# Reordering Q.K and P.V around the exponential in a 32-head attention kernel, with a shorter prologue and finish

## The chip, the cores and the metric

The kernel runs on one core of a Trainium2 chip. The metric is the device time of one launch in microseconds (us), measured over several launches; the profile is one further execution, whose span (first to last instruction) is about 1.8 us shorter than the timed value. Launches of one kernel agree within 0.13%.

Engines: TensorE does matrix products (PE in the profile, PEld its weight loads), ScalarE (ACT) the exponentials, VectorE (DVE) the small elementwise work, and the SyncE queue (SP) starts the DMA transfers.

## The reference

```python
B, H, S, D = 1, 32, 2048, 640      # Dh = D // H = 20
def reference(q, k, v, t):          # q, k, v: [1, 32, 2048, 20] bf16; t: [32]
    qn = q / (jnp.sqrt((q * q).sum(axis=-1, keepdims=True)) + 1e-6)
    kn = k / (jnp.sqrt((k * k).sum(axis=-1, keepdims=True)) + 1e-6)
    logits = jnp.einsum('bhqd,bhkd->bhqk', qn, kn) * t[None, :, None, None]
    attn = softmax(logits, axis=-1)
    return jnp.einsum('bhqk,bhkd->bhqd', attn, v)
```

Normalised rows make the logits small, so the kernel takes the exponential without subtracting a maximum. A column of ones beside V gives the denominators.

## The kernel before

The score matrix of a head (2048 keys x 2048 queries) is cut into 64 units of 128 keys x 512 queries. Three units make a *wave*: three Q.K matmuls write 3 x 512 columns of PSUM (`psS`, two slots), one activation takes the exponential of all 1536 columns into SBUF (`p_slot`, two slots), and three P.V matmuls add the result to the head's accumulator (`psO`). There are 683 waves. The heads have no gap between them: a wave may hold the end of one and the start of the next.

```python
def pe_qk(eng, w):                  # on TensorE
    slot = w % 2
    ...                             # first unit of a head: wait for the transposed q and k
    for i, uu in enumerate(us):
        ...
        last = eng.matmul(dst, lhsT, rhs, tile_position=(32 * g, 0))      # K = 20 rows
    last.then_inc(s_qk, 1)

def pe_pv(eng, w):
    ...                             # first unit of a head: zero its psO bank by a matmul with zeros
    eng.wait_ge(s_act, w + 1)       # activation w is done
    for i, uu in enumerate(us):
        ...
        last = eng.matmul(dst, lhsT, rhs, ..., tile_position=(0, 32 * g))  # 32 columns wide
    last.then_inc(s_pv, 1)

# ScalarE, for every wave w
eng.wait_ge(s_qk, w + 1)
eng.activation(p_slot[:, slot, ...], psS[slot ...], ACT.Exp).then_inc(s_act, 1)

# TensorE's program
for w in range(NW):
    pe_qk(eng, w)
    if w >= 1:
        pe_pv(eng, w - 1)
    if w in fin_at_wave:            # waves 4 to 7 of the next head:
        n, c = fin_at_wave[w]
        pe_fin_transposes(eng, n, c, c)   # four small transposes of head n's accumulator
```

Seen from the moment at which activation w-1 ends, TensorE does P.V(w-1), then perhaps four transposes, then Q.K(w+1). Activation w+1 needs that Q.K.

Per head, VectorE prepares q (square, sum, reciprocal square root in ten small steps, scale), then k in the same way with its own ten steps, and writes the normalised k four times into `kn_rep`; two DMA transposes then make `qTg` and `kT`. At the end of a head VectorE copies the accumulator to SBUF, TensorE transposes it back into PSUM, VectorE copies that to `fin_sb`, divides and stores.

Of the kernel before, what the change touches and what calls it, by code (L numbers as in the profile page):

```python
# [14 lines left out]
def bass_standalone__qk_norm__prompt_kernel(  # L15
# [28 lines left out]
    def first_wave_of_head(h):  # L44
        return (h * NU) // WAVE

    NB = 5
    NT = 2

    with ExitStack() as es:  # L50
# [10 lines left out]
        rqt_all = sbuf("rqt_all", [128, H, R], F32)  # L61
        rs_u = sbuf("rs_u", [128, R], I32)
        rs_a = sbuf("rs_a", [128, R], F32)
        rs_b = sbuf("rs_b", [128, R], F32)
        rs_c = sbuf("rs_c", [128, R], F32)
        rs_y = sbuf("rs_y", [128, R], F32)

# [10 lines left out]

        p_slot = sbuf("p_slot", [128, 2, WAVE * 512], BF16)

        acc_sb = sbuf("acc_sb", [128, 512], F32)
        fin_sb = sbuf("fin_sb", [128, 512], F32)
        rsum_rec = sbuf("rsum_rec", [128, R], F32)
# [10 lines left out]
        s_Tq = [sem(f"s_Tq{i}") for i in range(NT)]  # L94
        s_Tk = [sem(f"s_Tk{i}") for i in range(NT)]
        s_out = [sem(f"s_out{i}") for i in range(2)]
# [15 lines left out]
        def out_count_before(n):  # L112
            return n // 2

        def ld_count(n):
            return 16 * (n // NB + 1)

        def issue_loads(eng, n):
            b = n % NB
            if n >= NB:  # L120
                eng.wait_ge(s_pv, waves_done_through_head(n - NB))
            src_q = q[0, n].rearrange("(p r) d -> p r d", p=128)
            src_k = k[0, n].rearrange("(p r) d -> p r d", p=128)
            src_v = v[0, n].rearrange("(p r) d -> p r d", p=128)
            eng.dma_start(q_sb[b][:, :, :], src_q).then_inc(s_ldq[b], 16)
            eng.dma_start(k_sb[b][:, :, :], src_k).then_inc(s_ldk[b], 16)
            eng.dma_start(vaug[b][:, :, 0:D], src_v).then_inc(s_ldv[b], 16)

        def issue_transposes(eng, n):
            b = n % NB  # L130
            b2 = n % NT
            eng.wait_ge(s_prep, 2 * n + 1)
            if n >= NT:
                eng.wait_ge(s_qk, waves_done_through_head(n - NT))
            src = qn_pad[b][:, :, :].rearrange("p r d -> p (r d)")
            dst = qTg[b2][:, :].rearrange("p (c n) -> p c n", n=128)
            eng.dma_start_transpose(dst, src).then_inc(s_Tq[b2], 16)
            eng.wait_ge(s_prep, 2 * n + 2)
            src = kn_rep[b][:, :, :, :].rearrange("p r g d -> p (r g d)")
            dst = kT4[b2][:, :].rearrange("p (r n) -> p r n", n=128)  # L140
            eng.dma_start_transpose(dst, src).then_inc(s_Tk[b2], 16)

# [6 lines left out]
        @blk.sync  # L149
        def _(eng: bass.BassEngine):  # L150
            issue_loads(eng, 0)
            src_t = bass.AP(t.tensor, 0, [[0, 128], [1, H]])
            eng.dma_start(tb16[:, :], src_t).then_inc(s_tld, 16)
            if H > 1:
                issue_loads(eng, 1)
            for n in range(H):
                issue_transposes(eng, n)
                if n >= 2:
                    issue_out(eng, n - 2)
                if n + 2 < H:  # L160
                    issue_loads(eng, n + 2)
            for n in range(max(0, H - 2), H):
                issue_out(eng, n)
            n0 = (H + 1) // 2
            n1 = H // 2
            if n0 > 0:
                eng.wait_ge(s_out[0], 16 * n0)
            if n1 > 0:
                eng.wait_ge(s_out[1], 16 * n1)
# [6 lines left out]
        @blk.scalar  # L176
        def _(eng: bass.BassEngine):
            eng.wait_ge(s_init, 1)
            eng.activation(act_scr[:, :], act_scr[:, :], ACT.Exp)
            for w in range(NW):  # L180
                n_u = len(waves[w])
                slot = w % 2
                eng.wait_ge(s_qk, w + 1)
                src = psS[:, slot * WAVE * 512:slot * WAVE * 512 + n_u * 512]
                dst = p_slot[:, slot, 0:n_u * 512]
                eng.activation(dst, src, ACT.Exp).then_inc(s_act, 1)  # L186
# [45 lines left out]
        def dve_prep(eng, n):  # L232
            b = n % NB
            eng.wait_ge(s_ldq[b], ld_count(n))
            dve_wait_prev(eng)
            dop(eng, eng.tensor_tensor(sq_q[b][:, :, :], q_sb[b][:, :, :], q_sb[b][:, :, :], ALU.mult))  # L236
            dve_wait_prev(eng)
            dop(eng, eng.tensor_reduce(sums_all[:, n, 0:R], sq_q[b][:, :, :], AXIS_X, ALU.add))  # L238
            dve_rsqrt(eng, rinv_all[:, n, 0:R], sums_all[:, n, 0:R])
            if n == 0:  # L240
                eng.wait_ge(s_tld, 16)
                dve_wait_prev(eng)
                dop(eng, eng.tensor_copy(t_f32[:, :], tb16[:, :]))
            dve_wait_prev(eng)
            dop(eng, eng.tensor_scalar(rqt_all[:, n, :], rinv_all[:, n, 0:R],
                                      t_f32[:, n:n + 1], None, ALU.mult))
            dve_wait_prev(eng)
            rq = bcast_d(rqt_all[:, n, :])
            dop(eng, eng.tensor_tensor(qn_pad[b][:, :, 0:D], q_sb[b][:, :, :], rq, ALU.mult), ext=s_prep)  # L249
            eng.wait_ge(s_ldk[b], ld_count(n))  # L250
            dve_wait_prev(eng)
            dop(eng, eng.tensor_tensor(sq_k[b][:, :, :], k_sb[b][:, :, :], k_sb[b][:, :, :], ALU.mult))  # L252
            dve_wait_prev(eng)
            dop(eng, eng.tensor_reduce(sums_all[:, n, R:2 * R], sq_k[b][:, :, :], AXIS_X, ALU.add))  # L254
            dve_rsqrt(eng, rinv_all[:, n, R:2 * R], sums_all[:, n, R:2 * R])
            rk = bcast_d(rinv_all[:, n, R:2 * R])
            for g in range(NG):
                dve_wait_prev(eng)
                ins = eng.tensor_tensor(kn_rep[b][:, :, g, 0:D], k_sb[b][:, :, :], rk, ALU.mult)  # L259
                dve_chain(ins, ext=(s_prep if g == NG - 1 else None))  # L260

        def dve_fin(eng, n):
            b2 = n % 2
            eng.wait_ge(s_pv, waves_done_through_head(n))
            if n >= 1:
                eng.wait_ge(s_finT, 4 * n)
            dve_wait_prev(eng)
            dop(eng, eng.tensor_copy(acc_sb[:, :], psO[:, b2 * 512:(b2 + 1) * 512]), ext=s_fincopy)  # L268
            eng.wait_ge(s_finT, 4 * (n + 1))
            if n >= 2:  # L270
                eng.wait_ge(s_out[b2], 16 * out_count_before(n))
            dve_wait_prev(eng)
            dop(eng, eng.tensor_copy(fin_sb[:, :], psO[:, b2 * 512:(b2 + 1) * 512]))  # L273
            dve_wait_prev(eng)
            den = bass.AP(fin_sb, D, [fin_sb[:, :].ap[0], [32, R], [1, 1]])
            dop(eng, eng.reciprocal(rsum_rec[:, :], den))
            dve_wait_prev(eng)
            fin = bass.AP(fin_sb, 0, [fin_sb[:, :].ap[0], [32, R], [1, D]])
            rec_b = bass.AP(rsum_rec, 0, [rsum_rec[:, :].ap[0], [1, R], [0, D]])
# [33 lines left out]

        qk_waited_heads = set()
        pv_started_heads = set()

        def pe_qk(eng, w):
            slot = w % 2
            us = waves[w]
            for uu in us:  # L320
# [3 lines left out]
                if h not in qk_waited_heads:  # L324
                    eng.wait_ge(s_Tq[b2], 16 * (m2 + 1))
                    eng.wait_ge(s_Tk[b2], 16 * (m2 + 1))
                    qk_waited_heads.add(h)
            last = None
            for i, uu in enumerate(us):
# [8 lines left out]
        def pe_pv(eng, w):  # L338
# [14 lines left out]
            for i, uu in enumerate(us):  # L353
# [3 lines left out]
                lhsT = vaug[b][:, r, :]  # L357
                rhs = p_slot[:, slot, i * 512:(i + 1) * 512]
                dst = psO[32 * g:32 * g + 32, b2 * 512:(b2 + 1) * 512]
# [3 lines left out]

        def pe_fin_transposes(eng, n, g, chunk):
            b2 = n % 2
            if chunk == 0:
                eng.wait_ge(s_fincopy, n + 1)
            else:
                eng.wait_ge(s_finT, 4 * n + chunk)
            last = None  # L370
            for r in (g, g + 4, g + 8, g + 12):
                c = r // NG
# [7 lines left out]
        for n in range(H - 1):  # L380
            wb = first_wave_of_head(n + 1)
            for c in range(4):
                fin_at_wave[wb + 4 + c] = (n, c)

        @blk.tensor
        def _(eng: bass.BassEngine):
            for w in range(NW):
                pe_qk(eng, w)
                if w >= 1:
                    pe_pv(eng, w - 1)  # L390
                if w in fin_at_wave:
                    n, c = fin_at_wave[w]
                    pe_fin_transposes(eng, n, c, c)
            pe_pv(eng, NW - 1)
            for c in range(4):
                pe_fin_transposes(eng, H - 1, c, c)

# [27 lines left out]
```

## Time and profile before

The time before is 981.9 us. The following lines are from the page of the kernel before: the busy time of each engine (share of the span, number of instructions).

```profile
span 980.1 us, 11528 instructions
...
PE 832.1 (85%) x4640; PEld 198.5 (20%) x4640; DVE 333.0 (34%) x1115; ACT 935.7 (95%) x685; POOL 0.4 (0%) x5
```

The costliest groups of the kernel before. Columns: line, engine, operation, output<-inputs, shapes, count | busy us, mean ns of one | idle time of the engine just before them, and what ended it.

```profile
L186 ACT ACTIVATE p_slot<-psS 128x1536 bf16<-128x1536 f32 (+1 forms) x683 | 934.2, 1447 | 35.9 <-PE psS L335 31.1
L360 PE MATMUL psO<-p_slot,vaug 128*32 128x512 bf16 x2048 | 419.5, 608 | 126.7 <-ACT p_slot L186 125.4
L335 PE MATMUL psS<-qTg,kT 20*128 20x512 bf16 x2048 | 447.8, 602 | 16.6 <-DMA kT<-kn_rep 16.6
```

Up to the tail of 7.7 us, ScalarE's 683 activations fill the span except for 35.9 us, of which 15.0 are the start. TensorE, ahead of P.V, waits for ScalarE 125.4 us in all. The chain that ended last names TensorE too:

```profile
ACT 78%; PE 20%; DVE 1%; issue 1%; DMA 1%; ACTq 0%; DVEq 0%
```

Next, the timeline of the kernel before at a plain wave and at a wave with transposes (start us, duration us, engine, line, operation; in brackets the idle time before).

```profile
489.82 0.61 PE L360 MATMUL psO<-p_slot,vaug 128*32 128x512 bf16 x3 [0.21 <-ACT p_slot L186]
490.37 0.61 PE L335 MATMUL psS<-qTg,kT 20*128 20x512 bf16 x3
491.16 0.61 PE L360 MATMUL psO<-p_slot,vaug 128*32 128x512 bf16 x3 [0.18 <-ACT p_slot L186]
...
499.43 0.61 PE L360 MATMUL psO<-p_slot,vaug 128*32 128x512 bf16 x3 [0.18 <-ACT p_slot L186]
499.98 0.29 PE L376 MATMUL psO<-idn,acc_sb 21*128 21x21 f32 x1
499.99 0.61 PE L335 MATMUL psS<-qTg,kT 20*128 20x512 bf16 x2
500.10 0.48 PE L376 MATMUL psO<-idn,acc_sb 21*128 21x21 f32 x3
500.42 0.59 PE L335 MATMUL psS<-qTg,kT 20*128 20x512 bf16 x1
...
501.05 2.98 ACT L186 ACTIVATE p_slot<-psS 128x1536 bf16<-128x1536 f32 x2 [0.31 <-PE psS L335]
```

In a plain wave Q.K comes 0.55 us after P.V. With transposes its last matmul comes 0.99 us after P.V (500.42 against 499.43), and ScalarE stands idle for 0.31 us.

### The profile page before, as it was taken

To read this page: it belongs to the slowest core of one execution; us is meant where nothing else is said; L and a number is where in the kernel's file an instruction comes from. 1 tells how busy PE (TensorE), PEld (TensorE's weight loads), DVE (VectorE), ACT (ScalarE), POOL (GpSimd) and SP (SyncE) were. 2 spreads that over 40 slices of the span, in tenths; PEclk is the share of its full clock that TensorE was granted. 3 is DMA by queue.
4 is the path that set the end of the run, shared out by engine and by line. 5 is a ranking of instruction groups with operands and counts; after the bars stand their busy time and mean duration, and the time that the engine had idled before them with its cause. 6 is when DMAs were issued, how large, how long until landed. Compare 5 with 4: busy or idle time off the path is not lost.

```text
span 980.1 us, 11528 instructions
## 1 busy us (share of the span) xinstructions
PE 832.1 (85%) x4640; PEld 198.5 (20%) x4640; DVE 333.0 (34%) x1115; ACT 935.7 (95%) x685; POOL 0.4 (0%) x5
## 2 busy tenths in 40 slices
PE   2888888888888888888888888889888888888887
PEld 0122221222211222212222112222112222122221
DVE  8733134342234331334423343413343223430000
ACT  3999999999999999999999999999999999999996
POOL 0000000000000000000000000000000000000000
DMA  4212212122121122121221121321211222201100
GB/s 63 44 30 41 39 29 41 19 36 41 36 33 32 23 41 41 27 41 19 36 41 38 30 37 17 41 41 28 41 26 29 41 40 28 41 14 31 31 1 7
DMA packets 164037, 32.21 MB, mean 33 GB/s; under 512 B 151696, under 2 KB 163984, under 8 KB 163984
## 3 DMA queue, kind: packets, MB, share of 16 engines
q1 hardware_dynamic: 163984, 31.48, 19.5%
q8 instruction: 36, 0.59, 0.3%
q14 instruction: 17, 0.14, 0.1%
HBM read 7.87 MB, written 2.62 MB: 11 GB/s over the span
## 4 chain that ended last, share of the span: by engine, by line
ACT 78%; PE 20%; DVE 1%; issue 1%; DMA 1%; ACTq 0%; DVEq 0%
ACT p_slot L186 78%; PE psS L335 8%; PE psO L360 8%; PE psO L376 3%; PE psO L311 1%; DMA kT<-kn_rep 0%; DVE kn_rep L259 0%; DMA q_sb<-in_q_dram 0%; ACTq L50 0%; DVE rs_a L221 0%; DVE rs_b L223 0%; DVE rs_c L225 0%; DVE fin_sb L273 0%; DVE acc_sb L268 0%; DVE sq_q L236 0%
## 5 line engine op out<-in xcount | busy, mean ns | idle before, releaser
L186 ACT ACTIVATE p_slot<-psS 128x1536 bf16<-128x1536 f32 (+1 forms) x683 | 934.2, 1447 | 35.9 <-PE psS L335 31.1
L360 PE MATMUL psO<-p_slot,vaug 128*32 128x512 bf16 x2048 | 419.5, 608 | 126.7 <-ACT p_slot L186 125.4
L335 PE MATMUL psS<-qTg,kT 20*128 20x512 bf16 x2048 | 447.8, 602 | 16.6 <-DMA kT<-kn_rep 16.6
L360 PEld LDWEIGHTS psO<-p_slot,vaug 128*32 128x32 bf16 x2048 | 73.3, 101 | 461.2 <-ACT p_slot L186 461.2
L335 PEld LDWEIGHTS psS<-qTg,kT 20*128 20x128 bf16 x2048 | 90.1, 102 | 260.2 <-issue 260.2
L273 DVE COPY fin_sb<-psO 128x512 f32<-128x512 f32 x32 | 22.1, 692 | 281.0 <-PE psO L376 281.0
L268 DVE COPY acc_sb<-psO 128x512 f32<-128x512 f32 x32 | 22.1, 691 | 251.3 <-PE psO L360 251.3
L376 PE MATMUL psO<-idn,acc_sb 21*128 21x21 f32 x512 | 78.3, 276 | 1.0 <-DVE acc_sb L268 0.8
L376 PEld LDWEIGHTS psO<-idn,acc_sb 21*128 21x128 f32 x512 | 63.7, 209 | 56.0 <-issue 54.2
L259 DVE TENSOR_TENSOR kn_rep<-k_sb,rinv_all 128x320 bf16<-128x320 bf16 x128 | 63.0, 492 | 4.4
L236 DVE TENSOR_TENSOR sq_q<-q_sb 128x320 f32<-128x320 bf16 x32 | 15.8, 492 | 75.2 <-DMA q_sb<-in_q_dram 74.5
L223 DVE TENSOR_TENSOR rs_b<-rs_a,sums_all 128x16 f32<-128x16 f32 x128 | 22.3, 174 | 4.4
L225 DVE TENSOR_SCALAR rs_c<-rs_b 128x16 f32<-128x16 f32 x128 | 22.3, 174 | 4.4
L311 PE MATMUL psO<-zt 32*128 32x512 bf16 x32 | 19.9, 621 | 0.0
L252 DVE TENSOR_TENSOR sq_k<-k_sb 128x320 f32<-128x320 bf16 x32 | 15.7, 492 | 3.3
L249 DVE TENSOR_TENSOR qn_pad<-q_sb,rqt_all 128x320 bf16<-128x320 bf16 x32 | 15.7, 492 | 1.1
L281 DVE TENSOR_TENSOR o_stage<-fin_sb,rsum_rec 128x320 bf16<-128x320 f32 x32 | 15.7, 491 | 1.1
L238 DVE TENSOR_REDUCE sums_all<-sq_q 128x16 f32<-128x320 f32 x32 | 15.6, 486 | 1.1
L254 DVE TENSOR_REDUCE sums_all<-sq_k 128x16 f32<-128x320 f32 x32 | 15.5, 486 | 1.1
L221 DVE TENSOR_TENSOR rs_a<-rs_u 128x16 f32<-128x16 f32 x64 | 11.2, 175 | 2.2
L229 DVE TENSOR_TENSOR rs_y<-rs_u,rs_c 128x16 f32<-128x16 f32 x64 | 11.2, 174 | 2.2
L221 DVE TENSOR_TENSOR rs_a<-rs_y 128x16 f32<-128x16 f32 x64 | 11.2, 174 | 2.2
(21 smaller groups left out, 59.5 us busy)
## 6 DMA issues: line engine op xcount, KB each, us to landing
q_sb<-in_q_dram SPq DMA_DIRECT2D x32, 80.0 KB, 2.0
k_sb<-in_k_dram SPq DMA_DIRECT2D x32, 80.0 KB, 2.1
vaug<-in_v_dram SPq DMA_DIRECT2D x32, 80.0 KB, 3.1
out_dram<-o_stage SPq DMA_DIRECT2D x32, 80.0 KB, 1.6
qTg<-qn_pad SPq DMA_TRANSPOSE x32, 2.4
kT<-kn_rep SPq DMA_TRANSPOSE x32, 4.3
tb<-in_t_dram SPq DMA_DIRECT2D x1, 8.0 KB, 3.4
```

Source lines behind the costliest of these rows:

```text
L186: eng.activation(dst, src, ACT.Exp).then_inc(s_act, 1)
L221: dop(eng, eng.tensor_tensor(rs_a[:, :], cur, cur, ALU.mult))
L223: dop(eng, eng.tensor_tensor(rs_b[:, :], rs_a[:, :], src, ALU.mult))
L225: dop(eng, eng.tensor_scalar(rs_c[:, :], rs_b[:, :], -0.5, 1.5, ALU.mult, ALU.add))
L236: dop(eng, eng.tensor_tensor(sq_q[b][:, :, :], q_sb[b][:, :, :], q_sb[b][:, :, :], ALU.mult))
L259: ins = eng.tensor_tensor(kn_rep[b][:, :, g, 0:D], k_sb[b][:, :, :], rk, ALU.mult)
L268: dop(eng, eng.tensor_copy(acc_sb[:, :], psO[:, b2 * 512:(b2 + 1) * 512]), ext=s_fincopy)
L273: dop(eng, eng.tensor_copy(fin_sb[:, :], psO[:, b2 * 512:(b2 + 1) * 512]))
L311: eng.matmul(psO[:, b2 * 512:(b2 + 1) * 512], zt[0:32, 0:128], zt[0:32, 0:512], start=True, stop=True)
L335: last = eng.matmul(dst, lhsT, rhs, tile_position=(32 * g, 0))
L360: last = eng.matmul(dst, lhsT, rhs, start=False, stop=False, skip_group_check=True, tile_position=(0, 32 * g))
L376: last = eng.transpose(dst, lhsT, rhs, tile_position=(32 * g, 0))
```

## The change

The intent: keep ScalarE fed. (1) TensorE does Q.K(w) first after activation w-2 and P.V(w-2) behind it; P gets a third buffer, because activation w may now start before P.V(w-2) has read its input. (2) The transposes of a finished head are spread over eight waves, two in each. (3) The prologue of each head is shorter: q and k share one reciprocal square root, and k's transpose is split so that the first quarter can be used early; in the first head t is also loaded ahead of v. (4) The finish reads PSUM directly instead of through `fin_sb`. The core of the diff:

```diff
+    KA = 4
-        p_slot = sbuf("p_slot", [128, 2, WAVE * 512], BF16)
+        p_slot = sbuf("p_slot", [128, 3, WAVE * 512], BF16)
-                dst = p_slot[:, slot, 0:n_u * 512]
+                dst = p_slot[:, w % 3, 0:n_u * 512]
 ...                                                   # transposes: 2 in 8 waves, not 4 in 4
+            return [(g, g + 8) for g in range(NG)] + [(g + 4, g + 12) for g in range(NG)]
 ...                                                   # k's DMA transpose in two parts
+            src = kn_rep[b][:, 0:KA, :, :].rearrange("p r g d -> p (r g d)")
+            eng.dma_start_transpose(dst, src).then_inc(s_TkA[b2], 16)
+            src = kn_rep[b][:, KA:R, :, :].rearrange("p r g d -> p (r g d)")
+            eng.dma_start_transpose(dst, src).then_inc(s_TkB[b2], 16)
 ...                                                   # one root for q and k; k is squared first
-            dve_rsqrt(eng, rinv_all[:, n, 0:R], sums_all[:, n, 0:R])
+            dve_rsqrt(eng, rinv_all[:, n, :], sums_all[:, n, :])
 ...                                                   # kn_rep: two instructions in place of four
 ...                                                   # finish
-            dop(eng, eng.tensor_copy(fin_sb[:, :], psO[:, b2 * 512:(b2 + 1) * 512]))
-            den = bass.AP(fin_sb, D, [fin_sb[:, :].ap[0], [32, R], [1, 1]])
+            den = bass.AP(psO, b2 * 512 + D, [psO[:, :].ap[0], [32, R], [1, 1]])
 ...                                                   # TensorE's program
             for w in range(NW):
+                if w >= 2:
+                    eng.wait_ge(s_act, w - 1)
                 pe_qk(eng, w)
-                if w >= 1:
-                    pe_pv(eng, w - 1)
+                if w >= 2:
+                    pe_pv(eng, w - 2)
                 if w in fin_at_wave: ...
+            pe_pv(eng, NW - 2)
             pe_pv(eng, NW - 1)
```

In the program P.V appears one wave later. In time it does not: both orders wait for the same activation and then do one P.V and one Q.K. Only which of the two goes first is different.

More of the change, by code (lines that the diff above doesn't have):

```diff
@@ L61, in bass_standalone__qk_norm__prompt_kernel @@
         rqt_all = sbuf("rqt_all", [128, H, R], F32)
-        rs_u = sbuf("rs_u", [128, R], I32)
-        rs_a = sbuf("rs_a", [128, R], F32)
-        rs_b = sbuf("rs_b", [128, R], F32)
-        rs_c = sbuf("rs_c", [128, R], F32)
-        rs_y = sbuf("rs_y", [128, R], F32)
+        rs_u = sbuf("rs_u", [128, 2 * R], I32)
+        rs_a = sbuf("rs_a", [128, 2 * R], F32)
+        rs_b = sbuf("rs_b", [128, 2 * R], F32)
+        rs_c = sbuf("rs_c", [128, 2 * R], F32)
+        rs_y = sbuf("rs_y", [128, 2 * R], F32)
         q_sb = [sbuf(f"q_sb{i}", [128, R, D], BF16) for i in range(NB)]
@@ L77, in bass_standalone__qk_norm__prompt_kernel @@
         kT4 = [sbuf(f"kT4{i}", [128, R * 128], BF16) for i in range(NT)]
-        p_slot = sbuf("p_slot", [128, 2, WAVE * 512], BF16)
+        p_slot = sbuf("p_slot", [128, 3, WAVE * 512], BF16)
         acc_sb = sbuf("acc_sb", [128, 512], F32)
-        fin_sb = sbuf("fin_sb", [128, 512], F32)
         rsum_rec = sbuf("rsum_rec", [128, R], F32)
@@ L94, in bass_standalone__qk_norm__prompt_kernel @@
         s_Tq = [sem(f"s_Tq{i}") for i in range(NT)]
-        s_Tk = [sem(f"s_Tk{i}") for i in range(NT)]
+        s_TkA = [sem(f"s_TkA{i}") for i in range(NT)]
+        s_TkB = [sem(f"s_TkB{i}") for i in range(NT)]
         s_out = [sem(f"s_out{i}") for i in range(2)]
@@ L113, in out_count_before, with fin_chunks, fin_done_count, issue_loads @@
             return n // 2
+        def fin_chunks(n):
+            if n == H - 1:
+                return [(g, g + 4, g + 8, g + 12) for g in range(NG)]
+            return [(g, g + 8) for g in range(NG)] + [(g + 4, g + 12) for g in range(NG)]
+        fin_nchunks = [len(fin_chunks(n)) for n in range(H)]
+        def fin_done_count(n):
+            return sum(fin_nchunks[:n + 1])
         def ld_count(n):
             return 16 * (n // NB + 1)
-        def issue_loads(eng, n):
+        def issue_loads(eng, n, with_t=False):
             b = n % NB
@@ L126, in issue_loads @@
             eng.dma_start(k_sb[b][:, :, :], src_k).then_inc(s_ldk[b], 16)
+            if with_t:
+                src_t = bass.AP(t.tensor, 0, [[0, 128], [1, H]])
+                eng.dma_start(tb16[:, :], src_t).then_inc(s_tld, 16)
             eng.dma_start(vaug[b][:, :, 0:D], src_v).then_inc(s_ldv[b], 16)
@@ L131, in issue_transposes @@
             b2 = n % NT
-            eng.wait_ge(s_prep, 2 * n + 1)
+            eng.wait_ge(s_prep, 3 * n + 1)
             if n >= NT:
@@ L137, in issue_transposes @@
             eng.dma_start_transpose(dst, src).then_inc(s_Tq[b2], 16)
-            eng.wait_ge(s_prep, 2 * n + 2)
-            src = kn_rep[b][:, :, :, :].rearrange("p r g d -> p (r g d)")
-            dst = kT4[b2][:, :].rearrange("p (r n) -> p r n", n=128)
-            eng.dma_start_transpose(dst, src).then_inc(s_Tk[b2], 16)
+            eng.wait_ge(s_prep, 3 * n + 2)
+            src = kn_rep[b][:, 0:KA, :, :].rearrange("p r g d -> p (r g d)")
+            dst = kT4[b2][:, 0:KA * 128].rearrange("p (r n) -> p r n", n=128)
+            eng.dma_start_transpose(dst, src).then_inc(s_TkA[b2], 16)
+            eng.wait_ge(s_prep, 3 * n + 3)
+            src = kn_rep[b][:, KA:R, :, :].rearrange("p r g d -> p (r g d)")
+            dst = kT4[b2][:, KA * 128:R * 128].rearrange("p (r n) -> p r n", n=128)
+            eng.dma_start_transpose(dst, src).then_inc(s_TkB[b2], 16)
         def issue_out(eng, n):
@@ L150, in _ @@
         def _(eng: bass.BassEngine):
-            issue_loads(eng, 0)
-            src_t = bass.AP(t.tensor, 0, [[0, 128], [1, H]])
-            eng.dma_start(tb16[:, :], src_t).then_inc(s_tld, 16)
+            issue_loads(eng, 0, with_t=True)
             if H > 1:
@@ L233, in dve_prep @@
             b = n % NB
+            eng.wait_ge(s_ldk[b], ld_count(n))
+            dve_wait_prev(eng)
+            dop(eng, eng.tensor_tensor(sq_k[b][:, :, :], k_sb[b][:, :, :], k_sb[b][:, :, :], ALU.mult))
+            dve_wait_prev(eng)
+            dop(eng, eng.tensor_reduce(sums_all[:, n, R:2 * R], sq_k[b][:, :, :], AXIS_X, ALU.add))
             eng.wait_ge(s_ldq[b], ld_count(n))
@@ L249, in dve_prep @@
             dop(eng, eng.tensor_tensor(qn_pad[b][:, :, 0:D], q_sb[b][:, :, :], rq, ALU.mult), ext=s_prep)
-            eng.wait_ge(s_ldk[b], ld_count(n))
-            dve_wait_prev(eng)
-            dop(eng, eng.tensor_tensor(sq_k[b][:, :, :], k_sb[b][:, :, :], k_sb[b][:, :, :], ALU.mult))
-            dve_wait_prev(eng)
-            dop(eng, eng.tensor_reduce(sums_all[:, n, R:2 * R], sq_k[b][:, :, :], AXIS_X, ALU.add))
-            dve_rsqrt(eng, rinv_all[:, n, R:2 * R], sums_all[:, n, R:2 * R])
-            rk = bcast_d(rinv_all[:, n, R:2 * R])
-            for g in range(NG):
-                dve_wait_prev(eng)
-                ins = eng.tensor_tensor(kn_rep[b][:, :, g, 0:D], k_sb[b][:, :, :], rk, ALU.mult)
-                dve_chain(ins, ext=(s_prep if g == NG - 1 else None))
+            rk2 = rinv_all[:, n, R:2 * R]
+            for (r0, r1) in ((0, KA), (KA, R)):
+                nr = r1 - r0
+                dve_wait_prev(eng)
+                out4 = bass.AP(kn_rep[b], kn_rep[b][:, r0:r1, :, :].offset,
+                               [kn_rep[b][:, :, :, :].ap[0], [NG * 32, nr], [32, NG], [1, D]])
+                in0 = bass.AP(k_sb[b], k_sb[b][:, r0:r1, :].offset,
+                              [k_sb[b][:, :, :].ap[0], [D, nr], [0, NG], [1, D]])
+                in1 = bass.AP(rinv_all, rk2[:, r0:r1].offset, [rk2.ap[0], [1, nr], [0, NG], [0, D]])
+                dop(eng, eng.tensor_tensor(out4, in0, in1, ALU.mult), ext=s_prep)
         def dve_fin(eng, n):
@@ L265, in dve_fin @@
             if n >= 1:
-                eng.wait_ge(s_finT, 4 * n)
+                eng.wait_ge(s_finT, fin_done_count(n - 1))
             dve_wait_prev(eng)
             dop(eng, eng.tensor_copy(acc_sb[:, :], psO[:, b2 * 512:(b2 + 1) * 512]), ext=s_fincopy)
-            eng.wait_ge(s_finT, 4 * (n + 1))
+            eng.wait_ge(s_finT, fin_done_count(n))
             if n >= 2:
@@ L272, in dve_fin @@
             dve_wait_prev(eng)
-            dop(eng, eng.tensor_copy(fin_sb[:, :], psO[:, b2 * 512:(b2 + 1) * 512]))
-            dve_wait_prev(eng)
-            den = bass.AP(fin_sb, D, [fin_sb[:, :].ap[0], [32, R], [1, 1]])
+            den = bass.AP(psO, b2 * 512 + D, [psO[:, :].ap[0], [32, R], [1, 1]])
             dop(eng, eng.reciprocal(rsum_rec[:, :], den))
             dve_wait_prev(eng)
-            fin = bass.AP(fin_sb, 0, [fin_sb[:, :].ap[0], [32, R], [1, D]])
+            fin = bass.AP(psO, b2 * 512, [psO[:, :].ap[0], [32, R], [1, D]])
             rec_b = bass.AP(rsum_rec, 0, [rsum_rec[:, :].ap[0], [1, R], [0, D]])
@@ L314, in bass_standalone__qk_norm__prompt_kernel @@
         qk_waited_heads = set()
+        qk_waited_kparts = set()
         pv_started_heads = set()
@@ L325, in pe_qk @@
                     eng.wait_ge(s_Tq[b2], 16 * (m2 + 1))
-                    eng.wait_ge(s_Tk[b2], 16 * (m2 + 1))
                     qk_waited_heads.add(h)
+                key = (h, r < KA)
+                if key not in qk_waited_kparts:
+                    eng.wait_ge(s_TkA[b2] if r < KA else s_TkB[b2], 16 * (m2 + 1))
+                    qk_waited_kparts.add(key)
             last = None
@@ L357, in pe_pv @@
                 lhsT = vaug[b][:, r, :]
-                rhs = p_slot[:, slot, i * 512:(i + 1) * 512]
+                rhs = p_slot[:, w % 3, i * 512:(i + 1) * 512]
                 dst = psO[32 * g:32 * g + 32, b2 * 512:(b2 + 1) * 512]
@@ L362, in pe_pv, with pe_fin_transposes @@
             last.then_inc(s_pv, 1)
-        def pe_fin_transposes(eng, n, g, chunk):
+        def pe_fin_transposes(eng, n, m):
             b2 = n % 2
-            if chunk == 0:
+            if m == 0:
                 eng.wait_ge(s_fincopy, n + 1)
             else:
-                eng.wait_ge(s_finT, 4 * n + chunk)
+                eng.wait_ge(s_finT, fin_done_count(n - 1) + m)
+            rs = fin_chunks(n)[m]
+            g = rs[0] % NG
             last = None
-            for r in (g, g + 4, g + 8, g + 12):
+            for r in rs:
                 c = r // NG
@@ L381, in bass_standalone__qk_norm__prompt_kernel @@
             wb = first_wave_of_head(n + 1)
-            for c in range(4):
-                fin_at_wave[wb + 4 + c] = (n, c)
+            for m in range(fin_nchunks[n]):
+                fin_at_wave[wb + 4 + m] = (n, m)
         @blk.tensor
@@ L387, in _ @@
             for w in range(NW):
+                if w >= 2:
+                    eng.wait_ge(s_act, w - 1)
                 pe_qk(eng, w)
-                if w >= 1:
-                    pe_pv(eng, w - 1)
+                if w >= 2:
+                    pe_pv(eng, w - 2)
                 if w in fin_at_wave:
-                    n, c = fin_at_wave[w]
-                    pe_fin_transposes(eng, n, c, c)
+                    n, m = fin_at_wave[w]
+                    pe_fin_transposes(eng, n, m)
+            pe_pv(eng, NW - 2)
             pe_pv(eng, NW - 1)
-            for c in range(4):
-                pe_fin_transposes(eng, H - 1, c, c)
+            for m in range(fin_nchunks[H - 1]):
+                pe_fin_transposes(eng, H - 1, m)
 _INS = ['q', 'k', 'v', 't']
```

## The prediction

> **What bounds the kernel now.** ScalarE's exponentials: 683 activations, 934.2 of 980.1 us (list of costliest groups), 78% of the chain that ended last. Their start-to-start times in the trace fall into two kinds. 567 of 682 are 1.348 or 1.359 us in turn (mean 1.353): ScalarE itself, whose 1.45 us instructions overlap by 0.1. [...]The other 115 take 1.40 to 1.79 us and exceed the pace by 31.4 us in total, 1 us per head. They lie where TensorE has the zero matmul or four transposes of the previous head's accumulator between its P.V and its next Q.K (timeline). The span: 17.3 us to the first activation, 682 x 1.353 = 922.6, stalls 31.4, last activation 1.0, tail 7.7.
>
> **Why it stalls.** After activation w-1 ends, TensorE does P.V(w-1) (0.05 later), then Q.K(w+1) 0.54 after it, and activation w+1 can start 0.64 after that: 1.24 us of 1.26 available. Slack is 0.02, so four transposes (0.45 us) become a stall.
>
> **What the change does.**
> 1. P.V lags two waves; Q.K(w) waits only for activation w-2 and comes first after it: result ready 0.05 + 0.65 = 0.70 us after activation w-2 ends, slack 0.56. Work behind it hurts only if TensorE cannot keep 1.353 us per wave: Q.K to P.V about 0.52, P.V to transposes 0.54, two transposes (was four) 0.24: 1.30. It fits; the zero matmul's wave (1.6) overruns by 0.25 once a head, inside the slack. Nearly all 31.4 us should go.
> 2. Prologue. Now: q prep, k prep (two reciprocal square roots of ten 0.21 us steps), four 0.49 us writes of kn_rep, a whole k transpose, 4.3 us from issue to landing; first Q.K at 16.6. After: k lands about 3.3; four 0.52 us ops to 5.4; one root over 32 columns (10 x 0.226) to 7.6; scale and q write to 8.6; the q transpose keeps the queue until 9.95; the quarter k transpose, of the size of the q transpose (2.4 us), lands about 12.4. First activation near 13.05: -4.25 us. The other three quarters are needed at wave 5, 6 us later.
> 3. Tail: the 0.69 us copy of fin_sb goes: -0.7 us.
> 4. VectorE is relieved (10.4 us per head before), but is off the chain: worth nothing in the steady state.
>
> **Sum.** Span 13.05 + 922.6 + 1.0 + 7.0 + 0 to 3 residual = 944 to 947; timed about 1.8 more than the profiled span: 946 us (-3.6%). Range 942 to 955. Chances: faster by over 2% 0.93, within 2% 0.06, slower 0.01.
>
> **What would show it right or wrong.** ScalarE's idle before its main group, apart from the start: near zero, with "PE psS" as releaser gone. Starts 1.348/1.359 apart, also at head boundaries. First activation at 12.7 to 13.5. TensorE waits for ScalarE before Q.K instead of before P.V. Last activation to end: 7.0 us.
>
> **What would make it wrong.** TensorE not keeping the wave budget with two transposes[...]: delay would pile up over eight waves, leaving perhaps 0.3 us per head (10 us). ScalarE's own pace moving with the new phase of TensorE's writes: 0.01 us per wave is 7 us. The first k transpose queuing behind the q transpose: 1 to 2 us.

The 1.353 us is read from the trace, and the sum stays at a span of 944 to 947 us, 946 timed.

## The result, and the profile after

The kernel after takes 939.2 us (8 runs, 939.12 to 939.47) against 981.9 (13 runs): ratio 0.9565, 95% interval 0.9555 to 0.9574. Ratios here are the mean time of one kernel's fast runs over that of the other's of the same rounds, so not quite the ratio of the medians quoted. It is faster by 4.3%; 3.6% was forecast, and 939.2 lies 2.8 us below the range.

Busy times on the page of the kernel after:

```profile
span 937.4 us, 11176 instructions
...
PE 846.0 (90%) x4640; PEld 213.2 (23%) x4640; DVE 249.2 (27%) x699; ACT 918.7 (98%) x685; POOL 0.4 (0%) x5
```

The groups of the kernel after, and its chain by engine:

```profile
ACT 98%; DVE 1%; DMA 0%; PE 0%; issue 0%; ACTq 0%; SPq 0%; DVEq 0%
...
L202 ACT ACTIVATE p_slot<-psS 128x1536 bf16<-128x1536 f32 (+1 forms) x683 | 917.2, 1913 | 11.0 <-PE psS L357 11.0
L357 PE MATMUL psS<-qTg,kT 20*128 20x512 bf16 x2048 | 416.3, 603 | 87.1 <-ACT p_slot L202 72.8
L382 PE MATMUL psO<-p_slot,vaug 128*32 128x512 bf16 x2048 | 419.6, 608 | 0.5 <-ACT p_slot L202 0.5
```

ScalarE's only idle time ahead of the activations is the 11.0 us of the start. TensorE now waits for ScalarE ahead of Q.K (72.8) and no longer ahead of P.V (0.5). The chain is ScalarE's alone.

One number looks alarming: the mean of an activation rose from 1447 to 1913 ns, while the kernel became faster. The record of an activation now starts about 0.63 us before the one ahead of it ends, so records overlap, and their length is no longer work. The distances between *ends* give the pace. This table is worked out from the two traces (ns; waves of the same kind in each; "Q.K" is the start of Q.K(w) counted from the end of activation w-2, "P.V" the start of P.V(w) counted from the end of activation w; "4 T" and "2 T" are waves with four and with two transposes):

```
             wave  end to end   start - end of w-1   Q.K    P.V
before       145     1367             -84            600     52
before       146     1340            -104            599     53
before       147     1366             -85            599     53
before 4 T   154     1757             306            612     53
before 4 T   155     1530              79            881     53
after        146     1344            -629             55    597
after        147     1342            -627             55    594
after 2 T    134     1344            -481             55    596
after 2 T    135     1343            -494             55    593
```

In the kernel after, all 681 distances (the last, shorter activation left out) are 1.34 us, mean 1.343, whatever TensorE had to do in the wave. In the kernel before there are 115 long ones, together 32.8 us over 1.343, and the other 566 are not 1.343 either: they alternate between 1.340 and 1.366, which makes 5.0 us more.

In the "2 T" rows the records start only about 0.49 us early. That is not the doing of the transposes, for Q.K starts 55 ns after the activation's end there as elsewhere. These waves follow the zero matmul of the head's first P.V (wave 131), after which a record starts only 0.461 us early; from then on the starts are 1.331 us apart and win back 12 ns a wave.

The span in three stretches (us), from the traces:

| stretch | before | predicted | after |
|---|---|---|---|
| to the start of the first activation | 17.30 | 13.05 | 13.22 |
| first activation to the end of the last | 955.03 | 923.6 to 926.6 | 917.17 |
| end of the last activation to the end | 7.74 | 7.0 | 6.98 |
| sum | 980.07 | 944 to 947 | 937.4 |

The prologue and the tail came out within 0.2 us. The whole miss is in the middle.

The timeline of the kernel after at waves with two transposes, to be held against the one before:

```profile
191.24 0.61 PE L382 MATMUL psO<-p_slot,vaug 128*32 128x512 bf16 x3
191.79 0.40 PE L400 MATMUL psO<-idn,acc_sb 21*128 21x21 f32 x2
192.05 0.61 PE L357 MATMUL psS<-qTg,kT 20*128 20x512 bf16 x3
192.59 0.61 PE L382 MATMUL psO<-p_slot,vaug 128*32 128x512 bf16 x3
```

P.V to transposes 0.55 us, these to Q.K 0.26, Q.K to P.V 0.54: 1.35 us. This is ScalarE's pace and not TensorE's own time. In all 248 waves with transposes Q.K starts 54 to 56 ns after the end of the activation that it waits for, as in plain waves; TensorE was late in none of them. What TensorE itself needs for such a wave can't be read here (for an estimate see "Why the prediction was right or wrong").

### The profile page after: what moved, and what is told of

It is laid out like the page before. It is cut to its first block, busy times and chain, and to the rows that moved or that the text cites. A ratio compares the mean times of both kernels' runs of the same rounds, so it can differ in the third digit from the quotient of the medians.

```text
span 937.4 us, 11176 instructions
## 1 busy us (share of the span) xinstructions
PE 846.0 (90%) x4640; PEld 213.2 (23%) x4640; DVE 249.2 (27%) x699; ACT 918.7 (98%) x685; POOL 0.4 (0%) x5
## 4 chain that ended last, share of the span: by engine, by line
ACT 98%; DVE 1%; DMA 0%; PE 0%; issue 0%; ACTq 0%; SPq 0%; DVEq 0%
ACT p_slot L202 98%; PE psO L400 0%; DMA kT<-kn_rep 0%; DMA k_sb<-in_k_dram 0%; DVE kn_rep L280 0%; ACTq L51 0%; DVE acc_sb L288 0%; PE psS L357 0%; PE psO L382 0%; DVE sq_q L257 0%; DVE qn_pad L270 0%; DVE sq_k L252 0%; DVE sums_all L259 0%; DVE sums_all L254 0%; DVE o_stage L299 0%
## 5 line engine op out<-in xcount | busy, mean ns | idle before, releaser
L202 ACT ACTIVATE p_slot<-psS 128x1536 bf16<-128x1536 f32 (+1 forms) x683 | 917.2, 1913 | 11.0 <-PE psS L357 11.0
L357 PE MATMUL psS<-qTg,kT 20*128 20x512 bf16 x2048 | 416.3, 603 | 87.1 <-ACT p_slot L202 72.8
L357 PEld LDWEIGHTS psS<-qTg,kT 20*128 20x128 bf16 x2048 | 72.1, 99 | 304.5 <-ACT p_slot L202 291.9
L294 DVE RECIPROCAL rsum_rec<-psO 128x16 f32<-128x16 f32 x32 | 8.2, 257 | 374.3 <-PE psO L400 374.3
L400 PE MATMUL psO<-idn,acc_sb 21*128 21x21 f32 x512 | 101.2, 281 | 1.0 <-DVE acc_sb L288 0.8
L400 PEld LDWEIGHTS psO<-idn,acc_sb 21*128 21x128 f32 x512 | 72.4, 199 | 110.3 <-issue 108.5
L280 DVE TENSOR_TENSOR kn_rep<-k_sb,rinv_all 128x320 bf16<-128x320 bf16 x64 | 52.8, 825 | 2.2
L299 DVE TENSOR_TENSOR o_stage<-psO,rsum_rec 128x320 bf16<-128x320 f32 x32 | 15.7, 491 | 1.1
L239 DVE TENSOR_TENSOR rs_b<-rs_a,sums_all 128x32 f32<-128x32 f32 x64 | 12.3, 192 | 2.2
L241 DVE TENSOR_SCALAR rs_c<-rs_b 128x32 f32<-128x32 f32 x64 | 11.6, 181 | 2.2
```

What stands on the lines that cost most here:

```text
L202: eng.activation(dst, src, ACT.Exp).then_inc(s_act, 1)
L280: dop(eng, eng.tensor_tensor(out4, in0, in1, ALU.mult), ext=s_prep)
L299: dop(eng, eng.tensor_tensor(dst, fin, rec_b, ALU.mult), ext=s_findone)
L400: last = eng.transpose(dst, lhsT, rhs, tile_position=(32 * g, 0))
```

## The experiments

*Theory A*: each activation w of the kernel before waits on a loop through TensorE (end of activation w-2, P.V, Q.K, start of activation w). The loop spans two waves and has no slack at all, so it cost time in plain waves too; ScalarE's own pace is 1.343. From the trace of the kernel before (plain waves, us): end of activation w-2 to P.V 0.053, to the last Q.K matmul 0.554, to the start of activation w 0.649, its record 1.451. That is 2.707 for two waves, where ScalarE alone would need 2 x 1.343 = 2.687. *Rival B*: the third buffer makes something quicker. *Rival C*: relief of VectorE, split chunks or shorter reads help the steady state. *Rival D*: ScalarE's pace really was 1.353 while TensorE wrote PSUM at the old moments, and became 1.343 because these moments moved.

All twelve runs were timed in three rounds beside the kernel before. Names in b_ start from the kernel before, in a_ from the kernel after.

### The parts: b_slots3, b_order, a_oldorder, a_chunk4

b_slots3, the third buffer alone:

```diff
-        p_slot = sbuf("p_slot", [128, 2, WAVE * 512], BF16)
+        p_slot = sbuf("p_slot", [128, 3, WAVE * 512], BF16)
-                dst = p_slot[:, slot, 0:n_u * 512]
+                dst = p_slot[:, w % 3, 0:n_u * 512]
-                rhs = p_slot[:, slot, i * 512:(i + 1) * 512]
+                rhs = p_slot[:, w % 3, i * 512:(i + 1) * 512]
```

> The kernel before with a third p_slot buffer and nothing else. Theory A (the steady pace of the kernel before is set by the loop activation end, P.V, Q.K, activation start): a third buffer changes no wait, so 981.9 us, activation ends alternately 1.366 and 1.340 us apart as before. Rival B (ScalarE or TensorE run quicker because writing and reading of p_slot are spread over three buffers): the pace falls towards 1.3435 and about 6 to 7 us go, 975 us.

Measured: 981.89 against 981.85 us, ratio 1.000 (0.9985 to 1.0015); the mean end-to-end distance is 1.3989 as before. Rival B falls.

b_order, the third buffer and TensorE's order, with everything else as before:

```diff
             for w in range(NW):
+                if w >= 2:
+                    eng.wait_ge(s_act, w - 1)
                 pe_qk(eng, w)
-                if w >= 1:
-                    pe_pv(eng, w - 1)
+                if w >= 2:
+                    pe_pv(eng, w - 2)
 ...
+            pe_pv(eng, NW - 2)
             pe_pv(eng, NW - 1)
```

> The kernel before with Q.K put ahead of P.V after each activation (and the third p_slot that this needs); four-transpose chunks, prologue and tail as before. Theory A: all stalls and the thin wait of each second wave go, minus 37.7 us; but a wave with four transposes costs TensorE 0.54 + 0.55 + 0.47 = 1.56 us against a pace of 1.3435, four in a row pile up 0.86 us against 0.525 of slack, so some 0.3 us per head come back: 951 to 955 us. If TensorE's order were not the cause: above 975 us.

Measured: 945.75 us, ratio 0.9632 (0.9617 to 0.9646). The view of waits of b_order shows ScalarE waiting for Q.K once, at the start:

```profile
PE psS L335 <- ACT p_slot L186: 89.9, 472, 1.1
ACT p_slot L186 <- PE psS L335: 15.0, 1, 15.0
```

Of its 681 end-to-end distances all but 11 are 1.343; those 11 exceed it by 1.8 us together. The view doesn't list them: ScalarE's recorded idle time there is only 11 x 0.055 us, since the records overlap, so the ends have to be looked at. The order (with the buffer that it needs) thus brings 36.1 of the 42.7 us of span. The expectation was 5 to 9 us too high, because it reckoned that four transposes in a wave would cost more than they do (next run but one).

a_oldorder, the kernel after with only TensorE's order undone:

```diff
-                if w >= 2:
-                    eng.wait_ge(s_act, w - 1)
                 pe_qk(eng, w)
-                if w >= 2:
-                    pe_pv(eng, w - 2)
+                if w >= 1:
+                    pe_pv(eng, w - 1)
 ...
-            pe_pv(eng, NW - 2)
```

> The kernel after with P.V put ahead of Q.K again as in the kernel before; eight-chunk transposes, prologue, VectorE changes and tail as after. Theory A: the loop binds again, pace 1.353 and about 1 us of stalls per head return: 939.2 + 37.7 = 977 us, and the first activation stays at 13.2. Rival C (relief of VectorE, the split chunks or the shorter reads of the finish are what helps the steady state): 945 to 965 us.

Measured: 975.71 us, ratio 0.9937 (0.9922 to 0.9952). Its plain waves average 1.353 again and its long ones exceed 1.343 by 31.3 us. All the other parts of the change together are worth some 6 us without the order. Rival C falls. Another pair says the same: b_order and a_chunk4 (below) differ in VectorE's work and in the finish, and both take 918.93 us from the start of the first activation to the end of the last.

a_chunk4, the kernel after with four transposes in four waves:

```diff
-            return [(g, g + 8) for g in range(NG)] + [(g + 4, g + 12) for g in range(NG)]
+            return [(g, g + 4, g + 8, g + 12) for g in range(NG)]
```

> The kernel after with chunks of four transposes in four waves in place of two in eight. Theory A with the wave budget read from the trace of after (Q.K to P.V 0.54, P.V to transposes 0.55, 0.26 for two): four transposes make 1.56 us per wave, 0.22 over the pace, slack 0.525 used up in the third wave, 0.12 + 0.22 = 0.34 us stall per head: 949 us (946 to 951). Rival (the slack swallows it, as the slack of 0.56 in the prediction with 0.1 us per wave over would): 939.2 us.

Measured: 941.03 us, ratio 0.9584 (0.9568 to 0.96), so 1.8 us slower than the kernel after, where 10 had been reckoned. The trace shows why: the Q.K matmuls that use other row tiles than the transposes start among them instead of behind them (in one wave transposes at 46.86, 46.99, 47.10 and 47.20 us, Q.K at 47.12, 47.13 and, on the transposes' own row tile, 47.31). Only in one head of three (11 of 31) do four such waves follow each other at 1.513 us; they pile up 0.68 us against 0.525 us of slack, and ScalarE loses 0.16. The sum of 1.56 us had ignored this overlap. The split into eight chunks is thus worth 1.8 us, no more.

### Was the old pace ScalarE's own? b_pv448 and b_pv256

These two make the P.V matmuls of the kernel before shorter and change nothing else in its order. Their outputs are wrong, which doesn't matter for the times. The zero matmul starts the sums at 32. b_pv448:

```diff
-                rhs = p_slot[:, slot, i * 512:(i + 1) * 512]
-                dst = psO[32 * g:32 * g + 32, b2 * 512:(b2 + 1) * 512]
+                rhs = p_slot[:, slot, i * 512:i * 512 + 448]
+                dst = psO[32 * g:32 * g + 32, b2 * 512:b2 * 512 + 448]
 ...
-            dop(eng, eng.memset(zt[0:32, :], 0.0), ext=s_init)
+            dop(eng, eng.memset(zt[0:32, :], 1.0), ext=s_init)
```

> The kernel before with P.V on 448 of its 512 columns, a wrong result on purpose (the zero matmul starts the sums at 32 so that no denominator is zero). [...]Theory A (loop binds the steady pace): [...]the steady pace goes to about 1.3435 and 5 us go there[...]: 974 to 976 us. Rival D (1.353 was ScalarE's own pace in this phase of TensorE's writes): the steady pace stays, only slow waves shrink: 979 to 981 us.

> As b_pv448 with 256 of 512 columns[...]. Theory A: the steady pace does not fall further, since ScalarE itself holds it at 1.3435[...]: 968 to 971 us. Rival D: steady pace 1.353, 973 to 977 us. If the step does not shrink with the columns, both this and b_pv448 show nothing.

Measured: 971.34 us for 448 columns (ratio 0.989, 0.9875 to 0.9905) and 958.77 for 256 (ratio 0.9762, 0.9746 to 0.9779). From their traces (ns):

```
columns of P.V   Q.K after end of w-2   end to end, plain waves   excess of the long ones, us
512 (before)            600              1340 and 1366 in turn              32.8
448                     546              1343                               27.4
256                     387              1343                               14.1
```

The first 54 ns off the loop took the plain waves from a mean of 1.352 to 1.343; the next 159 ns took nothing more from them. That is what a loop does that binds by a hair: once it is shorter than ScalarE's own work, ScalarE sets the pace. The order and the number of matmuls were untouched, and Q.K still came behind P.V, some 0.55 us after an activation's end; rival D would have kept 1.353. It falls, for this much of a shift. The long waves kept shrinking with the columns, as they should.

The size was again off in the expectation: the times lie 3 and 9 us below it. The loop shrank by 54 ns for 64 columns and by 213 for 256, about 0.83 ns for each, which is more than the estimate that is cut had it.

### Has the new order slack? b_dup, a_dup, b_dup128, a_dup128

The first Q.K matmul of a wave is issued twice, with the same result, in 435 plain waves (those that hold transposes in the kernel after are left out in both):

```diff
                 last = eng.matmul(dst, lhsT, rhs, tile_position=(32 * g, 0))
+                if i == 0 and w not in no_dup:
+                    last = eng.matmul(dst, lhsT, rhs, tile_position=(32 * g, 0))
```

> The kernel before with the first Q.K matmul of a wave issued twice (same result) in all waves but the eight per head that hold transposes after the change: 435 waves get about 0.2 us more of TensorE work, all of them with TensorE idle for 0.2 us before. Theory A: the loop spans two waves and has no slack, so half of each 0.2 us shows: plus 35 to 48 us, 1017 to 1030 us. If TensorE's idle time of 0.2 us per wave were slack: 982 us.

> The same second matmul in the same 435 waves of the kernel after. Theory A: Q.K is ready 0.2 us later, of 0.525 us slack, and TensorE's wave of 0.54 + 0.54 + 0.2 = 1.29 us is under 1.3435: 939.2 us, up to 941. Activation ends stay 1.343 us apart.

Measured: 1078.05 us for b_dup (ratio 1.0975, 1.0959 to 1.0991) and 1006.58 for a_dup (ratio 1.0248, 1.0232 to 1.0263). Both missed: the dose was wrong. The second matmul starts 0.40 us after the first, not 0.2. (The 0.2 was the estimate, given without its source. The busy time of the kernel before comes to as little for each Q.K matmul, 447.8 us / 2048 = 0.22, but three of them share it there, starting 3 to 4 ns apart.) In b_dup the 435 waves then grow by 0.22 us each (95.9 us), half of the dose as a loop over two waves would have it; but each second of its plain waves takes 1.507 us, as in a_dup, so TensorE's own time may take part, and this pair alone proves little. In a_dup TensorE's own wave becomes 0.54 + 0.54 + 0.40 us; its plain waves end 1.507 apart, so TensorE bounds them. That shows the limit of the new order: it hides latency, not more work than 1.343 us per wave.

With a quarter of the columns:

```diff
+                if i == 0 and w not in no_dup:
+                    eng.matmul(dst[:, 0:128], lhsT, rhs[:, 0:128], tile_position=(32 * g, 0))
```

> b_dup with the second matmul on 128 of 512 columns. In b_dup the second matmul started 0.40 us after the first (twice what was reckoned) and each of the 435 waves grew by about half of that, 0.22 us, as a loop of two waves without slack would have it. A quarter of the columns: about 0.10 us of TensorE work, of which half shows. Theory A: 981.9 + 435 x 0.05 = 1004 us (1000 to 1008). If 0.1 us fitted into TensorE's idle 0.2 us per wave: 982 us.

> The same second matmul of 128 columns in the kernel after. a_dup cost 67 us because its wave of 0.54 + 0.54 + 0.40 = 1.507 us was over ScalarE's 1.3435: TensorE bound it. With 0.10 the wave is 1.19 us. Theory A: free, 939.2 us (up to 940), activation ends 1.343 us apart, the record of an activation starting about 0.5 us before the one ahead ends in place of 0.63.

Measured: 1004.1 us for b_dup128 (ratio 1.0226, 1.0209 to 1.0243), 939.42 for a_dup128 (ratio 0.9567, 0.9552 to 0.9581). The same matmuls cost 22 us in the old order. In the new they cost nothing: from the start of the first activation to the end of the last 917.17 us, as in the kernel after. In b_dup128 plain waves alternate between 1.340 and 1.473: the whole 0.107 us falls on each second wave, none on the other. In a_dup128 the activation ends stay 1.343 apart. The groups of a_dup128:

```profile
L202 ACT ACTIVATE p_slot<-psS 128x1536 bf16<-128x1536 f32 (+1 forms) x683 | 917.2, 1787 | 11.1 <-PE psS L357 11.1
...
L357 PE MATMUL psS<-qTg,kT 20*128 20x512 bf16 x2048 | 417.8, 603 | 48.1 <-DMA kT<-kn_rep 12.6 <-ACT p_slot L202 1.1
```

And of b_dup128:

```profile
L362 PE MATMUL psO<-p_slot,vaug 128*32 128x512 bf16 x2048 | 419.6, 608 | 107.3 <-ACT p_slot L186 88.3
```

Apart from the start (12.6 us), TensorE's idle time ahead of Q.K shrank from 74.5 us in the kernel after to 35.5, and ScalarE noticed nothing. (The view names a releaser only for gaps over 0.15 us. The gaps of about 0.19 us shrank to about 0.09, so only 1.1 us are put down to ScalarE; the rest is still there.) In b_dup128 TensorE still had 107.3 us of idle time ahead of P.V, against 126.7 in the kernel before, and yet each added matmul cost time. Idle time is not slack; where the work stands in the loop decides.

### Is the third buffer needed? a_slots2

```diff
-        p_slot = sbuf("p_slot", [128, 3, WAVE * 512], BF16)
+        p_slot = sbuf("p_slot", [128, 2, WAVE * 512], BF16)
 ...                                    # w % 3 becomes w % 2; on ScalarE:
                 eng.wait_ge(s_qk, w + 1)
+                if w >= 2:
+                    eng.wait_ge(s_pv, w - 1)
```

> The kernel after with two p_slot buffers; ScalarE then has to wait for P.V(w-2) before activation w overwrites its input. In after, P.V starts 0.60 us after its activation ends and its end is signalled about 0.65 later: 1.25 of 1.24 us available, so plain waves lose 0 to 0.01 us; in the wave with the zero matmul P.V starts 1.02 after, so about 0.43 us and part of the next wave are lost per head. Theory A: 939.2 + 13 to 25 = 952 to 965 us. If the third buffer were not needed for the gain: 939 to 941.

Measured: 978.55 us, ratio 0.9966 (0.9951 to 0.9981). Nearly all is lost, 14 us more than expected. Plain waves alternate between 1.341 and 1.425: the activation starts 0.715 us after the last P.V matmul in place of the 0.65 reckoned from the Q.K handoff. The direction was expected, the plain waves' loss was not. Whether the 0.065 us is the price of a second wait ahead of an instruction was not tested. The third buffer alone gains nothing (b_slots3), and the new order without it gains nothing either: from the start of the first activation to the end of the last it takes 956.5 us, against 955.0 in the kernel before; the 3.4 us that the run gains come from the prologue and the tail alone.

### A version that beats both: a_kfirst

The new prologue starts with k, but q is still loaded first. One swap:

```diff
-            eng.dma_start(q_sb[b][:, :, :], src_q).then_inc(s_ldq[b], 16)
             eng.dma_start(k_sb[b][:, :, :], src_k).then_inc(s_ldk[b], 16)
+            eng.dma_start(q_sb[b][:, :, :], src_q).then_inc(s_ldq[b], 16)
```

> An attempt to beat both: the kernel after with k loaded before q, since its prologue starts with k. k then lands some 0.45 us sooner, VectorE starts its chain at about 2.7 in place of 3.15, and everything to the first activation moves with it: first activation 12.8 in place of 13.2, 938.8 us.

Measured: 938.75 us (938.70 to 938.82), ratio 0.956 (0.9546 to 0.9574). The first activation starts at 12.79 us. It is correct and 0.5 us quicker than the kernel after, though against another set of runs of the kernel before; the two sets of launches do not overlap. The gain is no larger than the scatter of the prologue: other runs with the unchanged one have the first activation at 13.15 (a_oldorder) to 13.56 us (a_slots2).

## Why the prediction was right or wrong

- *ScalarE bounds the kernel, and the order is what lets it run*: right. The order and the buffer alone give 36.1 of 42.7 us (b_order), and without the order the rest gives 6 (a_oldorder).
- *"567 of 682 are 1.348 or 1.359 us in turn (mean 1.353): ScalarE itself"*: this is the step that failed. The 1.353 was the pace of the loop through TensorE; ScalarE itself takes 1.343, as the kernel after shows in every wave and b_pv448 shows in the old order. Counted against 1.343 the old kernel lost 37.8 us in the middle, not 31.4: 32.8 in long waves and 5.0 in plain ones. The difference of 6.4 us, and the allowance of up to 3 us for stalls left over, of which none was left, are the miss. The mechanism was right; this term of the sum was sized wrong. The prediction's list of risks does hold a change of ScalarE's pace by 0.01 us per wave (7 us), the right size, but for another reason (the phase of TensorE's writes, rival D).
- *"1.24 us of 1.26 available. Slack is 0.02"*: the same mistake in another place. In each second plain wave the activation started 0.649 us after the last Q.K matmul, much as in stalled waves (mostly 0.63 to 0.65); it was waiting. Ends that alternate by 26 ns could have been the hint: in the kernel after all ends are 1.339 to 1.345 us apart. The starts, alternating by 11 ns, were none, for they alternate by 7 ns in the kernel after too.
- *Slack 0.56 in the new order*: 0.525 measured (the record starts 0.629 before the end of its predecessor, 0.104 is the overlap in any case). The zero matmul's wave set Q.K back by 0.17 us (0.227 after the activation in place of 0.055), inside the slack, as said.
- *TensorE's wave of 1.30 us with two transposes*: it fits, as said, and nothing piled up. Its length can't be read from the kernel after, where these waves wait for ScalarE. An estimate from a_chunk4: where TensorE was late, waves with four transposes took 1.513 us and the plain wave after them 1.086, so a transpose adds 0.107 and two make 1.30.
- *Prologue -4.25 us*: -4.07. k landed at 3.13 us (about 3.3 was said) and the root ran from 5.32 to 7.60, 2.28 us (10 x 0.226 was the estimate); VectorE's chain reached the q write at 8.09 and the first quarter of k landed 2.5 us after its issue at 9.95. How much of it the shared root, the split and the order of loads bring each was read from the timeline only; no run separated the first two.
- *Tail -0.7 us*: -0.76.
- *VectorE's relief is worth nothing in the steady state*: right. 84 us less of VectorE's work left no trace in the activation ends (b_order against a_chunk4 above).

## What to carry to other kernels

Before calling a pace an engine's own, look for a loop that returns to it: if cutting a few tens of ns elsewhere in the loop makes the pace faster (54 ns in b_pv448: 1.352 to 1.343), the engine waits, and the recorded idle time understates the loss (here 21 us of idle time apart from the start stood for 37.8 us lost). In a loop of two engines, do first the work that the other engine waits for, and behind it the work that nobody waits for; buffers have to be there for that, and here neither the buffer nor the reordering gained anything without the other. Test slack by a dose: add a small, harmless instruction at the place in question; it should cost nothing where there is slack (a_dup128: 939.42 us against 939.21 without it; in b_dup128 it cost 22 us).
